# Products of k and v in four 64x64 quarters, over two PSUM banks

## The chip, the cores and the metric

The kernel runs on one core of a Trainium2 chip. The metric is the device time of one execution in microseconds (us). Before the change it is 837.13 us, the median of three runs (836.72 to 837.36).

## The reference, cut to what matters

```python
# batch 8, heads 8, seq 576, head_dim 64; x is (8, 576, 512)
kv = np.einsum('bhsd,bhse->bhde', k, v)
out = np.einsum('bhsd,bhde->bhse', q, kv)
rms = np.sqrt(np.mean(out * out, axis=-1, keepdims=True) + 1e-06)
x = (out / rms * g_norm)              # then heads side by side: 512 columns
...
h = x.transpose(0, 2, 1) @ U @ V      # rank 32, mixes along the sequence
u = x + h.transpose(0, 2, 1)
ch = np.maximum(u @ w_ch1, 0.0) @ w_ch2
return u + ch                         # all float32
```

The change touches only the first line, `k^T v`: a sum over 576 positions of the sequence, one 64x64 result for each of the 64 heads.

## The kernel before, in words

The 4608 tokens are nine blocks of 512. The first three (`NC`) go through `ffn1` (L480), `relu` (L491) and `ffn2` (L504) with each weight split into a high and a low part, three products for one. The other six go in three pairs through a seven-product scheme (`first_unit` L664, `second_unit` L761, order in `UNITS` L81); its weights are made during the first blocks by `weight_combos` (L608) and sent to DRAM on POOL's DMA queue (`wd`), together with plain copies of the weights (`weight_quarters` L593).

The attention part is spread between these products. A pair `(b, p)` is two heads of batch `b`. The table `RUNS` (L41) says behind which products `run` (L1061) is called; each call does one stage for three neighbouring pairs on TensorE, back to back: `t_product` of the pair before (L380; L387 and L390), `kv_product` of the next pair (L302, through `by_heads` at L294, matmul L300) and `out_product` of the pair itself (L310, matmul L319). Behind them the other engines do `t4_step` (L394), `kv_move` (L289), `squares` (L325), the statistics (L335) and `mul_step` (L358). `MIXES` (L46) places `mix_part` (L458), whose matmul L463 needs `t4`, some products later.

The order of TensorE is the order of the code (`manual_schedule`, L1139). The orders of DVE (VectorE), ACT (ScalarE), POOL (GpSimd) and SP (the DMA queue for loads and output) are set when the program is built, by a scheduler that works on its own estimates of how long each instruction takes. So a change to a few instructions can move others.

The two PSUM banks of a run are called `one` and `two` (in the trace `h` and `big`, or `pp` for both in the first three blocks). Columns 0 to 319 take `out_product`, one head in each bank, columns 320 to 447 of `two` the `t_product`, and columns 448 to 511 of one bank the 64x64 results of `kv_product`, head 0 in partitions 0 to 63 and head 1 in 64 to 127. `kv_move` copies them by ACT into `kvb` in SBUF, from where the next run's `out_product` takes them as the moving operand. Keys and values of a pair lie in SBUF as four tiles of 128 positions (`kv_sb`) and a tail of 64 (`kvt_sb`); for batches 2 to 7 the host pads the tail with 64 rows of zeros. A matmul in fp32 shows as two records, called passes here.

Of the kernel before, what the change touches and what calls it, by code (L numbers as in the profile page):

```python
# [16 lines left out]
ALU = mybir.AluOpType  # L17
AX = mybir.AxisListType

B, H, S, D = 8, 8, 576, 64  # L20
DM, DF, R = 512, 2048, 32
P = 128
NPAIR = H // 2
NT = 5
MAIN = 4 * P
TAIL = S - MAIN
# [4 lines left out]
BLK = 512  # L31
QL = [P + 32] * 2 + [P] * 2
QO = [0, 160, 320, 448]
ORDER = np.concatenate([np.arange(32) + P * i + 32 * a for a in range(4) for i in range(QL[a] // 32)])
NATIVE = 2
NC = 3
PAIRS = 3
KEEP = 4
# [54 lines left out]
def build(ctx: ExitStack, tc: tile.TileContext, kv_in, kvt0_in, kvt_in, q_in, uv_in, g_in, w_in, out):  # L93
    nc = tc.nc
# [25 lines left out]
    kvb = [const.tile([P, P], F32, name=f"kvb{i}") for i in range(2)]  # L120

    def weight_slot(name, shape, dtype, f):

        return const.tile(shape, dtype, name=name, tag=f"w_{f}")
# [51 lines left out]
    def move(which, n, out, in_, mul=None):  # L176

        e = ENG[which][n]
        if e == "a":
            if mul is None:  # L180
                nc.scalar.copy(out=out, in_=in_)
            else:
                nc.scalar.mul(out=out, in_=in_, mul=mul)
        else:
            eng = nc.vector if e == "v" else nc.gpsimd
            if mul is None:
                eng.tensor_copy(out=out, in_=in_)
            else:
                eng.tensor_scalar(out=out, in0=in_, scalar1=mul, scalar2=None, op0=ALU.mult)
# [9 lines left out]
    def load_kv(b, p):  # L199
        if b == 0 and 0 < p:  # L200
            if p not in first_kvq:
                first_kvq[p] = weight_slot(f"kvq{p}", [P, 2 * MAIN + S], F32, 8 + p)
            kt = first_kvq[p][:, 0:2 * MAIN]
        else:
            kt = ldp.tile([P, 2 * MAIN], F32, name="kv_sb")
        nc.sync.dma_start(out=kt, in_=kv_in[b, p])
        if b >= NATIVE:
            tt = ldp.tile([P, 2 * P], F32, name="kvt_sb")
            nc.sync.dma_start(out=tt, in_=kvt_in[b - NATIVE, p])
            loads["t", b, p] = tt  # L210
        elif p % 2 == 0:
            if b == 0 and p > 0:
                tt = temps[:, 2 * DM:2 * DM + 2 * P]
            else:
                tt = ldp.tile([P, 2 * P], F32, name="kvt_sb")
            nc.sync.dma_start(out=tt, in_=kvt0_in[b, p // 2])
            loads["t", b, p] = loads["t", b, p + 1] = tt
        loads["kv", b, p] = kt
# [65 lines left out]
    def banks():  # L284
        if "big" in second_y:
            return ps_h.tile([P, 512], F32, name="h"), second_y["big"].tile([P, 512], F32, name="big")
        return bank(), bank()

    def kv_move(b, p, pp):  # L289
        for lo in (0, D):  # L290
            own = slice(lo, lo + D)
            move("kv", p if b == 0 else -1, kvb[p % 2][own, own], pp[own])

    def by_heads(to, m, t, at):  # L294

        rows = slice(0, P) if at is None else slice(at, at + TAIL)
        for i in range(5):
            a, n = (m[:, i * P:], MAIN) if i < 4 else (t[rows], P)
            for lo in (0, D):
                nc.tensor.matmul(to[lo:lo + D], lhsT=a[:, lo:lo + D], rhs=a[:, n + lo:n + lo + D], start=i == 0, stop=i == 4)  # L300

    def kv_product(b, p, to):  # L302

        m = loads.pop(("kv", b, p))
        t = loads.pop(("t", b, p))
        by_heads(to, m, t, TAIL * (p % 2) if b < NATIVE else None)

    state = {}

    def out_product(b, p, heads):  # L310
        qt = loads.pop(("q", b, p))


        kb = kvb[p % 2]
        for i in range(NT):
            at = TAIL + i * P if i < 4 else 0
            for half in (0, D):
                for h, lo in enumerate((0, D)):
                    nc.tensor.matmul(heads[h][half:half + D, i * D:(i + 1) * D], lhsT=qt[lo:lo + D, at + half:at + half + D],  # L319
                                     rhs=kb[lo:lo + D, lo:lo + D], start=True, stop=True)  # L320
        x = x_sb[p % 2]
        state[b, p] = dict(x=x, x2=x, raw="two" in pools,
                           heads=[t[:, 0:NT * D].rearrange("p (i e) -> p i e", e=D) for t in heads])

    def squares(b, p):  # L325
        s = state[b, p]
        x = s["x"]
        for t, lo in zip(s["heads"], (0, D)):
            nc.scalar.activation(out=x[:, :, lo:lo + D], in_=t, func=AF.Copy if s["raw"] else AF.Square)
        if s["raw"]:  # L330
            xt = s["xt"] = sc.tile([P, 4, NT, 32], F32, name="xt")
            s["x2"] = xt.rearrange("p k i j -> p (k i j)").rearrange("p (i c) -> p i c", c=P)
            nc.scalar.activation(out=s["x2"], in_=x, func=AF.Square)
# [20 lines left out]
    def stats_step(b, p):  # L354
        for what in stats_parts(b, p).values():
            what()
# [27 lines left out]
    def t_product(b, p, tp):  # L384
        x = state[b, p]["x"]
        for i in range(4):
            nc.tensor.matmul(tp[R * i:R * (i + 1)], lhsT=uf[:, i, 0:R], rhs=x[:, i, :], start=True, stop=True)  # L387
        for i in range(2):
            cols = slice(i * D, (i + 1) * D)
            nc.tensor.matmul(tp[R * i:R * (i + 1), cols], lhsT=uf[:, 4, 0:R], rhs=x[:, 4, cols], start=False, stop=True,  # L390
                             skip_group_check=True)
        state[b, p]["tp"] = tp

    def t4_step(b, p):  # L394

        tp = state[b, p]["tp"]
        t4 = four.tile([P, P], F32R, name="t4")
        two = const.tile([2 * R, P], F32, name="two", tag="ident")
        other = sc.tile([2 * R, P], F32, name="other")
        nc.scalar.copy(out=two, in_=tp[2 * R:])  # L400
        nc.vector.tensor_tensor(out=two, in0=tp[0:2 * R], in1=two, op=ALU.add)
        for i in range(2):
            nc.scalar.copy(out=other[R * i:R * (i + 1)], in_=two[R * (1 - i):R * (2 - i)])
        nc.vector.tensor_tensor(out=two, in0=two, in1=other, op=ALU.add)
        nc.scalar.copy(out=t4[0:2 * R], in_=two)  # L405
        nc.vector.tensor_tensor(out=t4[2 * R:], in0=two, in1=t4[0:2 * R].bitcast(F32), op=ALU.subtract)
        state[b, p]["t4"] = t4
# [50 lines left out]
    def mix_part(b, p, part):  # L458
# [7 lines left out]
        if b > 2 and not (b in UPPER and part == 1):  # L466
            q = (S * b - BLK * NC) // (2 * BLK)
            at = S * b - BLK * NC - 2 * BLK * q
            to = x32(q)[p][:, at + lo:at + hi]
# [41 lines left out]
    def finish(y, j):  # L511
        uh, ul = ut[j]
        last_block = j == NC - 1
        kept = {}
# [27 lines left out]
    def x32(q):  # L542

        return [t[:, i] for t in x32_tiles(q) for i in range(2)]

    def carry(b, p):

        n = UPPER[b]
        q = (S * b + S - n - BLK * NC) // (2 * BLK)
        if b == 2:  # L550
# [161 lines left out]
    def end_unit(q, n, w):  # L712
# [17 lines left out]
        def leave(c, cols, queue):  # L730
            queue.dma_start(out=out[NC + 2 * q, 2 + c][:, cols], in_=ys[1][:, c, cols])

        if name != "P4":
            for c in range(2):
                products(c, slice(0, BLK), [(kk, w, hs)])
            if kk == KEEP - 1:
# [5 lines left out]
                if name == "P7":  # L742
                    nc.vector.tensor_tensor(out=ys[0], in0=ys[0], in1=spare("P5"), op=ALU.add)
                    for c in range(2):
                        nc.sync.dma_start(out=out[NC + 2 * q + 1, 2 + c], in_=ys[0][:, c])
            return
# [56 lines left out]
    uvraw = uvs[:, 0:NUV]  # L803
    nc.sync.dma_start(out=uvraw, in_=uv_in)
    load_kv(0, 0)
    load_q(0, 0)
    nc.vector.memset(eps[:, 0:1], 1e-6)
# [31 lines left out]
    for p in range(1, NPAIR):  # L839
        first[f"kv{p}"] = lambda p=p: load_kv(0, p)  # L840
        first[f"q{p}"] = lambda p=p: load_q(0, p)
# [60 lines left out]
    def spread_v(n, eng):  # L902
# [4 lines left out]
        out=uv, in_=uvraw.bitcast(U32).rearrange("p (n t) -> p n t", t=2)[:, :, 1].bitcast(F32), func=AF.Abs)  # L907
# [153 lines left out]
    def run(before, now, after):  # L1061

        one, two = banks()
        if before:
            t_product(*before, two[:, NT * D:NT * D + P])
        if after:
            kv = (two if after[0] < NATIVE and after[1] % 2 else one)[:, BLK - D:]
            kv_product(*after, kv)
        if now:
            out_product(*now, (one, two))  # L1070
        if before:
            t4_step(*before)
        if after:
            kv_move(*after, kv)
            following(load_kv, *after)
        if now:
            squares(*now)
            stats_step(*now)
            mul_step(*now)
            following(load_q, *now)  # L1080
            if now not in TURNS:
                turn_step(*now)

    def following(load, b, p):
        b, p = (b, p + 1) if p + 1 < NPAIR else (b + 1, 0)
        if b < B:
            load(b, p)
# [174 lines left out]
```

## Time and profile before

| | |
|---|---|
| median of three runs | 837.13 us (836.72 to 837.36) |
| the profiled execution | 837.33 us, its span 835.6 us |
| TensorE (PE) busy | 820.7 us, 98% |
| DVE busy | 585.4 us, 70% |
| ACT busy | 443.4 us, 53% |
| chain of work that ended last | PE 83%, DVE 6%, DMA 6%, ACT 3% |
| PE waits longer than 0.9 us past 50 us | 1.17 at 86.8, 3.42 at 98.4, 1.40 at 118.0, 0.94 at 536.6 |

The span is the profiled execution from its first to its last instruction. A row of a timeline gives the start and the duration, both in us, then engine, line, operation, the names written and read, shapes, and in brackets how long the engine had been idle before it and which instruction ended that. Time on an engine that nothing waits for costs nothing, so what a change is worth is read at the places where TensorE waits.

### The profile page before, as it was taken

To read this page: it belongs to the slowest core of one execution; us is meant where nothing else is said; L and a number is where in the kernel's file an instruction comes from. 1 tells how busy PE (TensorE), PEld (TensorE's weight loads), DVE (VectorE), ACT (ScalarE), POOL (GpSimd) and SP (SyncE) were. 2 spreads that over 40 slices of the span, in tenths; PEclk is the share of its full clock that TensorE was granted. 3 is DMA by queue.
4 is the path that set the end of the run, shared out by engine and by line. 5 is a ranking of instruction groups with operands and counts; after the bars stand their busy time and mean duration, and the time that the engine had idled before them with its cause. 6 is when DMAs were issued, how large, how long until landed. Compare 5 with 4: busy or idle time off the path is not lost.

```text
span 835.6 us, 14368 instructions
## 1 busy us (share of the span) xinstructions
PE 820.7 (98%) x5492; PEld 673.2 (81%) x5492; DVE 585.4 (70%) x1016; ACT 443.4 (53%) x810; POOL 80.3 (10%) x159
## 2 busy tenths in 40 slices
PE   8999799999999999999999999999999999999998
PEld 7777678888888888888888888788888888888887
DVE  5999885888776678666785688568736943582376
ACT  5978752544443445365645664656346724542462
POOL 3002214244330221000000000000000000000000
PEclk9999999999999999999999999999999999999999
DMA  9984767699887779467777768667555685555554
GB/s 346 415 340 144 225 200 226 219 321 277 262 252 266 239 214 316 160 236 262 241 264 236 264 238 282 231 204 242 178 187 196 207 281 197 182 196 195 202 200 153
DMA packets 66357, 198.39 MB, mean 237 GB/s; under 512 B 8176, under 2 KB 27376, under 8 KB 55536
## 3 DMA queue, kind: packets, MB, share of 16 engines
q1 hardware_dynamic: 57184, 167.97, 58.9%
q0 software_dynamic: 8960, 29.37, 10.5%
q8 instruction: 43, 0.70, 0.3%
q14 instruction: 26, 0.21, 0.1%
q10 hardware_dynamic: 144, 0.13, 0.0%
HBM read 146.84 MB, written 50.59 MB: 236 GB/s over the span
## 4 chain that ended last, share of the span: by engine, by line
PE 83%; DVE 6%; DMA 6%; ACT 3%; issue 1%; SPq 0%; ACTq 0%; DVEq 0%
PE yy L671 25%; PE yy L773 23%; PE y L508 13%; PE h L484 5%; PE h L485 5%; PE h L486 4%; DMA w1raw<-w_in 2%; PE ya L723 2%; DMA out<-x 1%; DMA raw<-w_in 1%; PE pp L300 1%; PE pp L319 1%; DVE dec L164 1%; PE h L300 1%; DVE uc L575 1%
## 5 line engine op out<-in xcount | busy, mean ns | idle before, releaser
L671 PE MATMUL yy<-uc,wt 128*128 128x512 f32 x1008 | 234.1, 391 | 0.9 <-ACT t L405 0.9
L671 PEld LDWEIGHTS yy<-uc,wt 128*128 128x128 f32 x1008 | 188.0, 188 | 40.7 <-ACT t L405 1.3
L773 PE MATMUL yy<-dec,wt 128*128 128x512 f32 x468 | 113.8, 391 | 0.3 <-DVE dec L662 0.3
L508 PE MATMUL y<-hh,ws 128*128 128x512 f32 x336 | 113.4, 393 | 0.0
L773 PE MATMUL yy<-hh,wt 128*128 128x512 f32 x312 | 103.3, 390 | 0.0
L773 PEld LDWEIGHTS yy<-dec,wt 128*128 128x128 f32 x468 | 87.2, 188 | 18.9 <-DVE dec L662 0.7
L662 DVE TENSOR_TENSOR hl<-hk,hh 128x512 fp32r<-128x512 f32 x72 | 48.1, 686 | 39.7 <-ACT hh L701 39.5
L662 DVE TENSOR_TENSOR dec<-hk,dec 128x512 fp32r<-128x512 f32 x72 | 48.9, 686 | 37.1 <-ACT dec L701 36.7
L508 PEld LDWEIGHTS y<-hh,ws 128*128 128x128 f32 x336 | 63.1, 188 | 13.8
L773 PEld LDWEIGHTS yy<-hh,wt 128*128 128x128 f32 x312 | 58.6, 188 | 12.4
L484 PE MATMUL h<-ut,ws 128*128 128x512 f32 x168 | 67.5, 402 | 0.0
L485 PE MATMUL h<-ut,ws 128*128 128x512 f32 x168 | 66.6, 396 | 0.0
L486 PE MATMUL h<-ut,ws 128*128 128x512 f32 x168 | 66.4, 395 | 0.0
L508 PE MATMUL y<-hl,ws 128*128 128x512 f32 x168 | 65.8, 391 | 0.0
L773 PE MATMUL yy<-hl,wt 128*128 128x512 f32 x156 | 60.7, 389 | 0.0
L701 ACT CAST dec<-hk 128x512 fp32r<-128x512 f32 x72 | 44.2, 621 | 29.0 <-PE yy L773 14.9
L701 ACT CAST hh<-hk 128x512 fp32r<-128x512 f32 x72 | 44.0, 622 | 27.0 <-PE yy L773 22.8
L659 ACT COPY sp<-yy 128x1024 f32<-128x1024 f32 x35 | 35.5, 1014 | 32.6 <-PE yy L671 25.3
L496 ACT ACTIVATE hh<-h 128x512 fp32r<-128x512 f32 x48 | 28.4, 591 | 36.8 <-PE h L486 36.6
L684 ACT ACTIVATE hk<-hk 128x1024 f32<-128x1024 f32 x24 | 25.5, 1061 | 36.3 <-DVE hk L683 36.3
L659 ACT COPY yy<-yy 128x1024 f32<-128x1024 f32 x17 | 17.0, 998 | 43.4 <-PE yy L671 40.5
L501 DVE SCALAR_TENSOR_TENSOR hl<-h,hh 128x512 fp32r<-128x512 f32 x48 | 32.7, 682 | 9.4 <-ACT hh L496 9.4
(237 smaller groups left out, 1348.0 us busy)
## 6 DMA issues: line engine op xcount, KB each, us to landing
wt<-wd SPq DMA_DIRECT2D x84, 1024.0 KB, 4.9
kv_sb<-kv_in SPq DMA_DIRECT2D x29, 512.0 KB, 5.9
raw<-w_in SPq DMA_DIRECT2D x14, 1023.6 KB, 14.9
wd<-dec POOLq DMA_DIRECT2D x44, 256.0 KB, 5.7
wd<-ws POOLq DMA_DIRECT2D x42, 256.0 KB, 4.0
q_sb<-q_in SPq DMA_DIRECT2D x29, 288.0 KB, 6.3
ut<-xd SPq DMA_DIRECT2D x28, 288.0 KB, 4.1
out<-x SPq DMA_DIRECT2D x23, 256.0 KB, 4.6
```

The lines of the kernel that those rows point to most:

```text
L484: nc.tensor.matmul(h, lhsT=w1s[f][0][:, d, :], rhs=uh[d], start=(n == 0), stop=False)
L485: nc.tensor.matmul(h, lhsT=w1s[f][0][:, d, :], rhs=ul[d], start=False, stop=False)
L486: nc.tensor.matmul(h, lhsT=w1s[f][1][:, d, :], rhs=uh[d], start=False, stop=(n == ND - 1))
L496: last["relu"] = nc.scalar.activation(out=last["hh"], in_=h, func=AF.Relu)
L501: last["low"] = nc.vector.scalar_tensor_tensor(out=hl, in0=h, scalar=0.0, in1=last["hh"].bitcast(F32), op0=ALU.max, op1=ALU.subtract)
L508: nc.tensor.matmul(acc, lhsT=w2s[f][w][:, c, :], rhs=h[:, cols], start=(f == 0 and w == 0 and h is hh), stop=(f == NF - 1 and w == 1))
L659: last["unit"] = nc.scalar.copy(out=pair_bank("P6") if name == "P1" else spare(name), in_=acc)
L662: return nc.vector.tensor_tensor(out=out, in0=a, in1=b, op=ALU.subtract)
L671: nc.tensor.matmul(acc[:, i], lhsT=w[:, ws_, e * P:(e + 1) * P], rhs=u[:, e, us], start=name in ("P1", "P5") and e == 0 and k == 0, stop=e ...
L684: last["unit"] = nc.scalar.activation(out=to, in_=to if other else acc, func=AF.Relu)
L701: last["unit"] = nc.scalar.copy(out=hh, in_=src)
L773: nc.tensor.matmul(acc[:, c], lhsT=w[:, ws_, c * P:(c + 1) * P], rhs=h, start=name in ("P1", "P5") and kk == 0 and i == 0, stop=kk == KEEP ...
```

## The change

`kv_product` of batches 2 to 7 (24 of the 32 pairs) goes through a new function `by_quarters`. Where `by_heads` did one matmul of 128 positions for each head and tile (a weight tile of 128x64), `by_quarters` does two of 64 positions each (weight tiles of 64x64): the upper rows go to bank `one`, the lower rows to bank `two`, four weight tiles side by side on the array. `kv_move` for these pairs copies the part in `one` to `kvb` by ACT and adds the part in `two` by DVE. The tails come without padding, 64 rows instead of 128. For batches 0 and 1 nothing changes.

```diff
+KV64 = 2
...
-            nc.sync.dma_start(out=tt, in_=kvt_in[b - NATIVE, p])
+            nc.sync.dma_start(out=tt[0:TAIL], in_=kvt_in[b - NATIVE, p])
...
     def kv_move(b, p, pp):
         for lo in (0, D):
             own = slice(lo, lo + D)
-            move("kv", p if b == 0 else -1, kvb[p % 2][own, own], pp[own])
+            if b >= KV64:
+                nc.scalar.copy(out=kvb[p % 2][own, own], in_=pp[0][own])
+                nc.vector.tensor_tensor(out=kvb[p % 2][own, own], in0=pp[1][own], in1=kvb[p % 2][own, own], op=ALU.add)
+            else:
+                move("kv", p if b == 0 else -1, kvb[p % 2][own, own], pp[own])
...
-        rows = slice(0, P) if at is None else slice(at, at + TAIL)
+        rows = slice(at, at + TAIL)
...
+    def by_quarters(to, m, t):
+
+        for i in range(5):
+            a, n = (m[:, i * P:], MAIN) if i < 4 else (t, P)
+            for r in (0, 1) if i < 4 else (0,):
+                rows = slice(r * D, (r + 1) * D)
+                for lo in (0, D):
+                    nc.tensor.matmul(to[r][lo:lo + D], lhsT=a[rows, lo:lo + D], rhs=a[rows, n + lo:n + lo + D], start=i == 0,
+                                     stop=i == (3 if r else 4))
...
-        by_heads(to, m, t, TAIL * (p % 2) if b < NATIVE else None)
+        if b >= KV64:
+            by_quarters(to, m, t)
+        else:
+            by_heads(to, m, t, TAIL * (p % 2))
...
-            kv = (two if after[0] < NATIVE and after[1] % 2 else one)[:, BLK - D:]
+            kv = [t[:, BLK - D:] for t in (one, two)]
+            kv = kv if after[0] >= KV64 else kv[after[1] % 2]
...
-    def padded(a):
-        n = B - NATIVE
-        a = tail_of(a[NATIVE:]).reshape(n, NPAIR, TAIL, P)
-        return np.concatenate([a, np.zeros_like(a)], axis=2)
+    def tails(a):
+        return tail_of(a[NATIVE:]).reshape(B - NATIVE, NPAIR, TAIL, P)
```

On TensorE the order only gains the new matmuls. On the other engines it moves at three places that the prediction speaks of; line numbers of the changed kernel are higher, by 1 near the top, by 18 from `kv_move` on.

The first place is ACT about 105 us into the program, where weight chunks are being decoded (`dec<-raw` is the first copy of a decode, `top<-dec` the second, `hh<-h` the relu). Before, and then now:

```order
L422 ACTIVATE ut<-ut_90,g_sb 128x448 [waits DMAHW5_49,DVE_49]
L167 COPY dec<-raw_1035 128x1024 [waits DMAHW7_49,DMAHW2_49,DVE_49]
L496 ACTIVATE hh<-h 128x512 [waits PE_49,Pool_49]
L168 COPY top<-dec 128x1024 [waits DVE_49]
L258 CAST ws_1382<-dec 128x1024 [waits DVE_49]
L168 COPY top<-dec 128x1024 [waits DVE_49,Activation_49]
```

```order
L440 ACTIVATE ut<-ut_90,g_sb 128x448 [waits DMAHW4_49,DVE_49]
L514 ACTIVATE hh<-h 128x512 [waits PE_49,Pool_49]
L168 COPY dec<-raw_1035 128x1024 [waits DMAHW7_49,DMAHW2_49,DVE_49]
L169 COPY top<-dec 128x1024 [waits DVE_49]
L259 CAST ws_1392<-dec 128x1024 [waits DVE_49]
L169 COPY top<-dec 128x1024 [waits DVE_49,Activation_49]
```

The relu now stands ahead of the copy `dec<-raw` and waits for TensorE there.

The second place is ACT at about 195 us, around a run (`kvb`, `two`, `x`, `other`, `xt`, `t` belong to it). `dec` and `sh` of `st` are the rounding of weight combinations in `weight_combos`; `sh` waits for POOL's earlier DMAs out of the same buffer. Before, and then now:

```order
L496 ACTIVATE hh<-h 128x512 [waits PE_49,Pool_49]
L628 CAST dec<-st 128x2x256 [waits DMASW6_49,DMASW5_49,DVE_49]
L181 COPY kvb_100<-pp 64x64 [waits PE_49]
L400 COPY two<-pp 64x128 [waits PE_49,Activation_49]
L628 CAST dec<-st 128x2x256 [waits DMASW3_49,DMASW2_49,DVE_49]
L181 COPY kvb_100<-pp 64x64
L329 ACTIVATE x_88<-pp 128x5x64
L403 COPY other<-two 32x128 [waits DVE_49]
L403 COPY other<-two 32x128
L329 ACTIVATE x_88<-pp 128x5x64
L333 ACTIVATE xt<-x_88 128x640 [waits DMAHW2_49,DMAHW1_49,DMAHW3_49,DMAHW0_49,Activation_49]
L405 CAST t_2319<-two 64x128 [waits DVE_49]
```

```order
L514 ACTIVATE hh<-h 128x512 [waits PE_49,Pool_49]
L646 CAST dec<-st 128x2x256 [waits DMASW6_49,DMASW5_49,DVE_49]
L646 CAST dec<-st 128x2x256 [waits DMASW7_49,DMASW0_49,DVE_49]
L646 CAST sh<-st 128x2x256 [waits DMASW4_49,DMASW5_49,DVE_49,Activation_49]
L294 COPY kvb_100<-pp 64x64 [waits PE_49]
L418 COPY two<-pp 64x128 [waits PE_49]
L294 COPY kvb_100<-pp 64x64
L347 ACTIVATE x_88<-pp 128x5x64
L421 COPY other<-two 32x128 [waits DVE_49]
L421 COPY other<-two 32x128
L347 ACTIVATE x_88<-pp 128x5x64 [waits DVE_49]
L351 ACTIVATE xt<-x_88 128x640 [waits DMAHW2_49,DMAHW1_49,DMAHW3_49,DMAHW0_49,Activation_49]
```

Now two roundings stand ahead of the run's first `kvb`, the second of them the `sh` that before came four rows behind `t_2319`, with its wait. POOL's DMAs behind the copy `begun` change their order at the same place. Before, and then now:

```order
L1158 COPY begun<-hh 128x1 [waits Activation_49]
L597 DMA wd_131<-ws_1210 128x2x256 [waits DMASW4_49]
L597 DMA wd_133<-ws_1210 128x2x256 [waits DMASW5_49]
L631 DMA wd_118<-sh 128x512 [waits DMASW6_49,DVE_49]
L631 DMA wd_118<-sh 128x512 [waits DMASW7_49]
L597 DMA wd_134<-ws_1263 128x2x256 [waits DMASW0_49]
```

```order
L1177 COPY begun<-hh 128x1 [waits Activation_49]
L649 DMA wd_118<-sh 128x512 [waits DMASW4_49,DVE_49]
L649 DMA wd_118<-sh 128x512 [waits DMASW5_49]
L615 DMA wd_131<-ws_1210 128x2x256 [waits DMASW6_49]
L615 DMA wd_133<-ws_1210 128x2x256 [waits DMASW7_49]
L615 DMA wd_134<-ws_1263 128x2x256 [waits DMASW0_49]
```

The two stores out of `sh` now go ahead of the two out of `ws_1210`.

The third place is DVE at about 536 us, in the middle of the first pair of blocks. `hk<-yy,sp` (L683 before, L701 now) takes a finished bank of `first_unit` to SBUF; `two`, `sums`, `t` and `r` belong to a run. Before, and then now:

```order
L662 TENSOR_TENSOR hl<-hk,hh 128x512 [waits Activation_49] x2
L401 TENSOR_TENSOR two<-big,two 64x128 [waits Activation_49]
L404 TENSOR_TENSOR two<-two,other 64x128 [waits DVE_49,Activation_49]
L683 TENSOR_TENSOR hk<-yy,sp 128x1024 [waits PE_49]
L348 TENSOR_REDUCE sums<-xt 128x10 [waits Activation_49]
L406 TENSOR_TENSOR t_5683<-two,t_5683 64x128 [waits Activation_49]
L683 TENSOR_TENSOR hk<-yy,sp 128x1024 [waits PE_49]
L351 RECIPROCAL r_5705<-ta 128x10 [waits Activation_49]
```

```order
L680 TENSOR_TENSOR hl<-hk,hh 128x512 [waits Activation_49] x2
L419 TENSOR_TENSOR two<-big,two 64x128 [waits Activation_49]
L295 TENSOR_TENSOR kvb_99<-big,kvb_99 64x64
L295 TENSOR_TENSOR kvb_99<-big,kvb_99 64x64 [waits Activation_49]
L422 TENSOR_TENSOR two<-two,other 64x128 [waits DVE_49,Activation_49]
L366 TENSOR_REDUCE sums<-xt 128x10 [waits Activation_49]
L424 TENSOR_TENSOR t_5911<-two,t_5911 64x128 [waits Activation_49]
L369 RECIPROCAL r_5935<-ta 128x10 [waits Activation_49]
L701 TENSOR_TENSOR hk<-yy,sp 128x1024 [waits PE_49]
```

`hk` now stands behind `sums`, `t` and the reciprocal, which waits for ACT's square root `ta` of `sums`. The two `kvb` rows are the new additions.

## Rows read from the trace of the kernel before

**Rows 1.** Section 1 of the page: busy time, share of the span, instructions.

```profile
PE 820.7 (98%) x5492; PEld 673.2 (81%) x5492; DVE 585.4 (70%) x1016; ACT 443.4 (53%) x810; POOL 80.3 (10%) x159
```

**Rows 2.** Timeline of PE: start, us, instruction, [idle before <-releaser]; four places.

```profile
101.78 0.58 PE L463 MATMUL pp<-v,t 128*128 128x288 f32 x1 [3.42 <-DVE t L406]
...
119.42 0.37 PE L463 MATMUL pp<-v,t 128*128 128x288 f32 x1 [1.40 <-DVE t L406]
205.45 0.33 PE L463 MATMUL pp<-v,t 128*128 128x384 f32 x1
...
537.58 0.70 PE L671 MATMUL yy<-uc,wt 128*128 128x512 f32 x2 [0.94 <-ACT t L405]
```

**Rows 3.** Busy time by windows; PEclk is the granted clock.

```profile
100.70:107.50 6.80, 5.72 (x14) 4.28 (x14) 6.59 (x17) 4.18 (x5) 2.36 (x4) 0.50 0.59 199
```

**Rows 4.** Timeline of PE in one run, 353.35 to 353.75.

```profile
353.35 0.29 PE L300 MATMUL h<-kvt_sb 128*64 128x64 f32 x4
353.56 0.27 PE L319 MATMUL h<-kvb,q_sb 64*64 64x64 f32 x1
...
353.67 0.22 PE L319 MATMUL h<-kvb,q_sb 64*64 64x64 f32 x1
...
353.73 0.22 PE L319 MATMUL h<-kvb,q_sb 64*64 64x64 f32 x1
```

**Rows 5.** Timeline of PE, run with a 64-row tail, at 73.4.

```profile
73.42 0.27 PE L300 MATMUL pp<-kvt_sb 64*64 64x64 f32 x2
73.44 0.28 PE L319 MATMUL pp<-kvb,q_sb 64*64 64x64 f32 x2
```

**Rows 6.** Timeline of ACT, 105 to 109.

```profile
105.40 1.15 ACT L167 COPY dec<-raw 128x1024 uint8<-128x1024 uint8 x1 [1.22 <-DMA wf<-dec]
107.77 0.60 ACT L496 ACTIVATE hh<-h 128x512 fp32r<-128x512 f32 x1 [1.22 <-PE h L486]
108.26 1.35 ACT L168 COPY top<-dec 128x1024 uint8<-128x1024 uint8 x1
```

**Rows 7.** Timeline of DVE, at 110.

```profile
110.34 1.21 DVE L164 SCALAR_TENSOR_TENSOR dec<-raw,top 128x1024 uint32<-128x1024 uint32 x1
```

**Rows 8.** Timeline of DVE, at 201.

```profile
201.07 0.28 DVE L406 TENSOR_TENSOR t<-two,t 64x128 fp32r<-64x128 f32 x1
```

**Rows 9.** Timeline of ACT, 195 to 204.

```profile
195.88 0.20 ACT L181 COPY kvb<-pp 64x64 f32<-64x64 f32 x1 [2.09 <-PE pp L319]
...
197.04 0.62 ACT L628 CAST dec<-st 128x512 fp32r<-128x512 f32 x1 [0.67 <-DVE st L622]
...
203.26 0.62 ACT L628 CAST sh<-st 128x512 fp32r<-128x512 f32 x1 [1.21 <-DMA wd<-sh]
```

**Rows 10.** Timeline of POOL, 193 to 196: issue of DMAs.

```profile
193.69 1.45 POOL L597 DMA_DIRECT2D wd<-ws  x2
195.14 1.11 POOL L631 DMA_DIRECT2D wd<-sh  x2
```

**Rows 11.** Timeline of DVE, 536 to 540.

```profile
536.06 0.28 DVE L404 TENSOR_TENSOR two<-two,other 64x128 f32<-64x128 f32 x1 [0.67 <-ACT other L403]
536.27 1.21 DVE L683 TENSOR_TENSOR hk<-yy,sp 128x1024 f32<-128x1024 f32 x1
537.40 0.80 DVE L348 TENSOR_REDUCE sums<-xt 128x10 f32<-128x640 f32 x1
...
539.69 0.21 DVE L351 RECIPROCAL r<-ta 128x10 f32<-128x10 f32 x1
```

**Rows 12.** Timeline of ACT, 536 to 539.

```profile
536.52 0.74 ACT L333 ACTIVATE xt<-x 128x640 f32<-128x640 f32 x1
...
538.48 0.29 ACT L349 ACTIVATE ta<-sums,eps 128x10 f32<-128x10 f32 x1
```

**Rows 13.** Chain of waits, 500 to 545: start, us, what.

```profile
519.69 7.10 DMA out<-x
```

**Rows 14.** Section 6 of the page: DMA issues, KB each, median us to landing.

```profile
out<-x SPq DMA_DIRECT2D x23, 256.0 KB, 4.6
```

More of the change, by code (lines that the diff above doesn't have):

```diff
@@ L1240 @@
         "kvt0_in": np.concatenate([tail_of(kk[:NATIVE]), tail_of(vv[:NATIVE])], axis=3),
-        "kvt_in": np.concatenate([padded(kk), padded(vv)], axis=3),
+        "kvt_in": np.concatenate([tails(kk), tails(vv)], axis=3),
         "q_in": np.concatenate([qq[:, :, :, MAIN:], qq[:, :, :, :MAIN]], axis=3).transpose(0, 1, 2, 4, 3).reshape(B, NPAIR, P, S),
```

## The prediction, made before the run

> **What bounds the kernel now.** I read the busy times of the page first: TensorE (PE) is busy for 820.7 of 835.6 us [rows 1]. So two things can move the end: the length of PE's own stream, and the few places where PE waits. For these I went through the timeline of PE for rows with idle time before them. Of the long ones three lie where the change reaches: 3.42 us before 101.78, 1.40 before 119.42 and 0.94 before 537.58 [rows 2]. The first two wait for `t` of DVE's L406, which ends a run's chain. The third is put down to ACT's `t`, which belongs to another matmul; what ended last before it is DVE's `hk` (536.27 + 1.21 = 537.48) [rows 11], which empties a bank that PE writes next. The row at 205.45 is an L463 that does not wait today.
>
> Then the granted clock by stretches [rows 3]. [...] Behind the 1.40 us idle it was up: the same L463 took 0.37 there, and 0.58 behind the 3.42 [rows 2]. So one idle of 3.42 us cost its own length and then 6.8 us at half speed, which is 3.4 us of work.
>
> **The change, part by part.**
>
> *Matmuls.* A row with x4 of L300 at 353.35 is two rounds of two records (the two heads, side by side); L319 has rounds of four, at 353.56, 353.67 and 353.73 [rows 4]. An ordinary round takes 0.06 us, with two tiles or with four. Between the last round of L300 (353.41) and the first of L319 stand 0.15, and the next takes 0.11: where the weight tile changes from 128x64 to 64x64, PE loses about 0.10 + 0.05 = 0.15 us. Where L300 has a 64x64 tile already, the tail in the run at 73.4, L319 begins 0.02 behind it, with no gap [rows 5]. In the change L300 has L319's tile shape throughout, so of two changes of shape per run one goes: 24 runs by 0.15 = 3.6 us saved. The rounds stay ten: five tiles by two passes for the upper rows, four by two for the lower, now four records a round instead of two.
>
> [...]
>
> *Additions.* 48 adds of 64x64 on DVE. The nearest row is `t` at 201.07, 64x128 in 0.28 [rows 8]; nothing is one bound, 0.28 the other, I take 0.2, about 10 us of DVE, which is 70% busy [rows 1]. In the order they stand between the first `two` of a run and the second, and in that stretch DVE waits for ACT's `other` anyway, 0.67 us at 536.06 [rows 11]. Without that cover each run's `t` would come up to 0.56 later, which matters only at the three places below.
>
> *Tails.* 24 loads of 64 KB instead of 128 KB, early loads nobody waits for: nothing.
>
> *First place, 119.42.* `hh` at 107.77 waits for PE, and the copy `dec<-raw` (1.15 us), which stood before it at 105.40, now stands behind it [rows 6]. So that copy runs from 108.26 to 109.41, and `top<-dec` (1.35) to 110.76. DVE's L164 needs it and begins at 110.98 instead of 110.34 [rows 7]: 0.65 later. From there to `t` at 119.42 it is one chain: each idle stretch that DVE has on the way was ended by an ACT step on the same chain. PE waits 0.65 longer. Bounds: nothing, if the wait for `hh` ends earlier, and 1.15, the whole copy.
>
> *Second place, 205.45.* The rounding of `sh`, which stood behind the run at 203.26 and there waited for POOL's stores, now stands ahead of the run's `kvb`, and so does the rounding at 197.04 [rows 9]. From `kvb` (195.88) to the end of `t` (201.35) are 5.47 us; without the rounding and the wait before it (0.62 + 0.67) 4.2 are left. So `t` is ready 0.62 + 4.2 = 4.8 after the stores out of `sh` have landed, and PE wants it at about 205.3. Before, they were issued at 195.14 behind two other stores (1.45) and had landed by 203.26 [rows 9, 10]. If they land as then, PE waits 2.9. If they gain the 1.45 by which they go ahead of the other stores, they land at 201.8 and PE waits 1.4. If they land by 200.4, it does not wait. A rounding is moved ahead of an earlier run as well and makes the engines later, which takes back some of the gain. I take 1.5, the middle; bounds 0 and 2.9.
>
> *Third place, 537.58.* `hk` (1.21) began at 536.27, ahead of `sums`; now it stands behind `sums`, `t` and the reciprocal, which need ACT's `xt` and `ta` [rows 11, 12]. `xt` ends at 537.26, `sums` takes 0.80, `ta` 0.29, the reciprocal 0.21, `hk` 1.21, with handovers it ends at about 539.8 instead of 537.48. PE waits 2.35 longer. The lower bound is nothing, if ACT's chain comes that much earlier (a rival); the upper adds two additions, 0.4.
>
> *Clock.* The third wait grows to 0.94 + 2.35, and 0.15 more because PE arrives earlier: 3.4 us, as long as the one idle that brought the clock down. I count it as a second fall, 3.4 us. Bounds: 0 and 3.4.
>
> *What the waits swallow.* In the three runs at those places the 0.15 saved only lengthens a wait: 21 runs by 0.15 = 3.15 are left.
>
> **Sum**, against the profiled execution (837.33, its span 835.6, 0.2 above the median of 837.13): -3.15 + 0.65 + 1.5 + 2.35 + 3.4 = +4.75. From the median that makes **841.9 us**. With 0 to 2.9 at the second place and 0.5 either way for the rest: 840.2 to 843.5.
>
> **Rivals.**
>
> *The clock stays up at 537.* Everything else as above: +1.35, 838.5, with the second place's bounds 837.0 to 840.0. For it: 1.40 us of idle did not bring the clock down, and there is only one idle of 3.4 to go by. Against it: the forecast's wait is just that long.
>
> *The clock falls at 119 too.* There the idle grows from 1.40 to 2.2, and only 12 us before, the clock was down. It would add 1.7 to 3.4: 843.6 to 845.3, with the bounds up to 847. For it: in the 3.42 us idle the clock was down before PE had work again; against it: the 1.40 us idle left no trace.
>
> *The other side: the output store lands early.* The chain that leads to the `hk` at 536 goes back to a store of `x` to the output, issued at 519.69 and landed 7.10 us later [rows 13], while the median of the 23 of its kind is 4.6 [rows 14]. The tail loads are smaller and some loads move, so it may land like the median, 2.5 us earlier. From 2.35 earlier on the third place adds nothing, PE's wait there stays at about 0.94, and the clock stays up. Then -3.15 + 0.65 = -2.5 without a wait at the second place: 834.6, faster. A wait there takes it back: with 1.5 it is 836.1, and from 0.9 on the change is within 0.2%. Against it: nothing in the order touches that store itself.
>
> *Quarters not side by side.* The change would not do what it says on the array. If each of the 36 records took half a round of L300, 0.029, a pair would take 1.04 instead of 0.58; 24 by 0.46 = 11 more: about 853. The rows of L319 speak against it. [...]
>
> **How the numbers follow.** Forecast 0.42, clock up at 537 0.25, clock down at 119 too 0.11, store early 0.17, quarters one by one 0.05. The predicted time is the forecast's, 841.9. About 1.7 us, 0.2%, is what a measurement of this kernel tells from no change: faster is below 835.5, slower above 838.8. Of the store rival 0.12 is faster, where the second place waits under 0.9, and 0.05 within 0.2%. Of the rival with the clock up two thirds lie within 0.2%: 0.17, together 0.22. All else is slower: 0.66. The range leaves out the faster part of the store rival and the rival on the quarters, and takes in the bounds of the others: 836.0 to 846.0. The likeliest case's own is 840.2 to 843.5.
>
> **What would show it.** L300 to L319 in the timeline of PE: no 0.15 between them, ten rounds of 0.06. PE's idle before L463 near 119: 2.2. Before L463 near 205: about 1.5, with ACT's `sh` ahead of `kvb` named by a `wd<-sh` store. Before L671 near 537: 3.4 behind DVE's `hk`, and a granted clock of 0.50 for some 7 us behind it. I would be wrong on the sign if that wait is missing, or if the clock stays at 1.00 there and the second place does not wait.

## The result, and the profile after

The changed kernel took 845.16 us (median of 7 runs, 840.2 to 845.93) beside 837.13 us for the kernel before (836.72 to 837.73): a ratio of 1.0083, 95% interval 1.0061 to 1.0105. It is slower, by 8.0 us where 4.8 was forecast. The profiled execution of it took 845.76 us with a span of 844.0. One execution of an experiment below (halves in the new order) had a mean granted clock of 0.65, took 1157.82 us, and is left out of its ratio.

The page's busy times of the changed kernel, and its chain by engine:

```profile
PE 820.5 (97%) x5876; PEld 672.3 (80%) x5876; DVE 595.6 (71%) x1064; ACT 443.1 (53%) x810; POOL 80.2 (9%) x159
...
PE 68%; DVE 12%; DMA 10%; ACT 4%; issue 3%; SPq 1%; POOL 1%; ACTq 0%; DVEq 0%; POOLq 0%
```

PE is busy as long as before [rows 1] although 384 records were added. What grew is the time in which it waits, and the chain shows it: PE's share falls from 83% to 68%, DVE's and the DMAs' grow from 6% each to 12% and 10%. The waits on PE from 50 us on, with the releaser, the total, how many and the longest:

```profile
PE pp L481 <- DVE t L424: 7.0, 3, 3.0
PE yy L689 <- issue: 3.5, 1, 3.5
PE pp L405 <- DVE x L381: 2.2, 2, 1.2
PE y L526 <- DVE hl L519: 1.8, 3, 0.9
PE y L526 <- ACT hh L514: 1.1, 1, 1.1
```

Before there were two waits for `t`, one of 1.2 for `x` and one of 0.9. Their places, in the timeline of PE:

```profile
100.85 0.37 PE L481 MATMUL pp<-v,t 128*128 128x288 f32 x1 [2.83 <-DVE t L424]
...
106.71 0.42 PE L405 MATMUL pp<-x,uf 128*32 128x128 f32 x8 [1.06 <-DVE x L381]
...
118.13 0.37 PE L481 MATMUL pp<-v,t 128*128 128x288 f32 x1 [1.20 <-DVE t L424]
...
159.66 0.50 PE L526 MATMUL y<-hl,ws 128*128 128x512 f32 x1 [0.95 <-DVE hl L519]
...
187.37 0.50 PE L526 MATMUL y<-hh,ws 128*128 128x512 f32 x1 [1.10 <-ACT hh L514]
188.10 0.50 PE L526 MATMUL y<-hl,ws 128*128 128x512 f32 x1 [0.22 <-DVE hl L519]
...
209.91 0.41 PE L481 MATMUL pp<-v,t 128*128 128x384 f32 x1 [2.97 <-DVE t L424]
...
348.45 0.50 PE L526 MATMUL y<-hl,ws 128*128 128x512 f32 x1 [0.66 <-DVE hl L519]
...
544.63 0.47 PE L689 MATMUL yy<-uc,wt 128*128 128x512 f32 x1 [3.52 <-issue]
```

The second place (209.91) and the third (544.63) wait for about 3 us and more; the first (118.13) less than before [rows 2]. Four rows stand where there was no wait: 106.71, 159.66, 187.37 with 188.10, and 348.45.

The granted clock, by windows behind three of them (the column ahead of the last two):

```profile
102.20:105.60 3.40, 3.40 (x9) 2.15 (x7) 3.03 (x8) 1.85 (x3) 0.83 (x2) 0.50 0.95 311
...
211.40:214.80 3.40, 3.40 (x10) 2.66 (x9) 3.37 (x6) 0.61 (x1) 1.11 (x2) 0.50 0.84 286
545.90:549.30 3.40, 3.40 (x10) 2.63 (x9) 3.02 (x3) 1.34 (x2) 0.00 (x0) 0.50 0.15 33
```

While PE had work left it fell three times for 3.4 us each, where before it fell once for 6.8 [rows 3]. The shorter stretch at 102 is not shown to come from the change: the length differs between executions. The kernel of the additions alone, below, has no quarters and the order of before, and its trace has 3.4 us there too:

```profile
101.40:104.70 3.30, 3.30 (x10) 2.63 (x10) 3.23 (x9) 2.07 (x4) 1.90 (x3) 0.50 0.86 293
104.80:108.10 3.30, 2.84 (x69) 2.13 (x72) 3.30 (x8) 2.78 (x3) 0.00 (x0) 1.00 0.30 101
```

Where the time went is read best from the start of the same matmul in both traces. How much later it starts in the changed kernel, in us:

| stretch of the changed kernel | later at its end | what moved it |
|---|---|---|
| to 101 | -0.9 | the wait at 98 is 0.6 shorter, the rest from the first 20 us |
| to 105 | -2.1 | the clock at half speed for 3.4 us less |
| at 107 | -0.9 | the new wait for `x` takes 1.2 back |
| 118 to 158 | -1.5 | runs, and the first place 0.2 shorter |
| at 160 | -0.3 | the new wait for `hl` |
| at 188 | +1.4 | the new waits for `hh` and `hl` |
| at 210 | +4.5 | the second place |
| to 215 | +6.3 | the clock |
| to 347 | +4.8 | eight runs at -0.19 |
| at 348 | +5.6 | the new wait for `hl` |
| to 541 | +4.5 | runs at -0.19, a wait of 0.5 at 535 |
| at 545 | +7.0 | the third place |
| to 550 | +8.6 | the clock |
| end | +8.4 | the last run |

The saving itself is there in every run. The timeline of PE in one run of the changed kernel:

```profile
267.09 0.69 PE L314 MATMUL pp<-kv_sb 64*64 64x64 f32 x32
267.61 0.23 PE L314 MATMUL pp<-kvt_sb 64*64 64x64 f32 x2
267.62 0.27 PE L337 MATMUL pp<-kvb,q_sb 64*64 64x64 f32 x2
267.67 0.23 PE L314 MATMUL pp<-kvt_sb 64*64 64x64 f32 x2
267.72 0.75 PE L337 MATMUL pp<-kvb,q_sb 64*64 64x64 f32 x38
```

Thirty-two records of quarters take 0.52 us, the tail's two rounds begin at 267.61 and 267.67, and L337 begins at 267.62, 0.01 behind the first of them: `out_product` already runs beside the tail, which has two tiles a round where the quarters have four. The 0.15 of [rows 4] are gone and 0.04 more; 24 runs by 0.19 are 4.5 us.

### The profile page after: what moved, and what is told of

Read it like the earlier page. It is cut to its first block, busy times and chain, and to the rows that moved or that the text cites. A ratio compares the mean times of both kernels' runs of the same rounds, so it can differ in the third digit from the quotient of the medians.

```text
span 844.0 us, 15183 instructions
## 1 busy us (share of the span) xinstructions
PE 820.5 (97%) x5876; PEld 672.3 (80%) x5876; DVE 595.6 (71%) x1064; ACT 443.1 (53%) x810; POOL 80.2 (9%) x159
## 4 chain that ended last, share of the span: by engine, by line
PE 68%; DVE 12%; DMA 10%; ACT 4%; issue 3%; SPq 1%; POOL 1%; ACTq 0%; DVEq 0%; POOLq 0%
PE yy L689 25%; PE yy L791 22%; PE y L526 7%; PE h L502 3%; PE h L504 2%; PE h L503 2%; DMA w1raw<-w_in 2%; PE ya L741 2%; DMA xd<-xt 2%; DMA out<-x 2%; DMA raw<-w_in 1%; DVE hl L519 1%; DVE uc L593 1%; DVE dec L165 1%; DMA wd<-dec 1%
## 5 line engine op out<-in xcount | busy, mean ns | idle before, releaser
L689 PE MATMUL yy<-uc,wt 128*128 128x512 f32 x1008 | 235.5, 392 | 4.0 <-issue 3.5
L689 PEld LDWEIGHTS yy<-uc,wt 128*128 128x128 f32 x1008 | 189.1, 189 | 44.1 <-issue 3.9
L526 PEld LDWEIGHTS y<-hl,ws 128*128 128x128 f32 x168 | 31.8, 190 | 9.5 <-DVE hl L519 3.5
```

What stands on the lines that cost most here:

```text
L526: nc.tensor.matmul(acc, lhsT=w2s[f][w][:, c, :], rhs=h[:, cols], start=(f == 0 and w == 0 and h is hh), stop=(f == NF - 1 and w == 1))
L689: nc.tensor.matmul(acc[:, i], lhsT=w[:, ws_, e * P:(e + 1) * P], rhs=u[:, e, us], start=name in ("P1", "P5") and e == 0 and k == 0, stop=e ...
```

## The experiments

**How the order was put back.** The order of DVE, ACT, POOL and SP in the changed kernel differs from that before in some thirty places of two to fourteen instructions. Edges that set the issue order alone, without a wait, put it back, so that TensorE's part and the order can be tried apart. The edit, cut to the chain of one place on one engine; numbers are positions in the order in which the code emits an engine's instructions:

```diff
+CHAINS = dict(
...
+    ACT=[[591, 600, 597, 598, 601]],
...
+)
...
     rest.close()
+    names = dict(DVE=mybir.EngineType.DVE, ACT=mybir.EngineType.Activation, POOL=mybir.EngineType.Pool, SP=mybir.EngineType.SP)
+    for name, chains in CHAINS.items():
+        own = [i for i in nc.cur_bb.bb.instructions if i.engine == names[name] and not type(i).__name__.startswith(("BassTile", "InstTile"))]
+        for chain in chains:
+            for a, b in zip(chain, chain[1:]):
+                tc.add_manual_dep(own[b], own[a].name, mybir.DependencyInfo(mybir.DependencyClass.NoSync, mybir.DependencyReason.DATA), reason="order")
```

The chain shown is ACT's at the third place, as the kernel under "One place back" has it; the others have such lists for DVE, ACT, POOL and SP. In the traces of the kernels with all chains the instructions of the four engines, apart from the additions, do stand in the order before, or in the new one. Gains and losses below are told by the ratios to the kernel before, since not all runs were on one chip.

**All places back.** All chains (42), on the changed kernel.

> The changed kernel with the order of the kernel before put back on DVE, ACT, POOL and SP by edges between instructions (the 48 additions stand behind the first `two` of their run); TensorE as changed. Theory A, the order alone costs: the quarters save 0.19 us a run as in the trace of the changed kernel, 24 runs, 4.6 us, of which the three old waits swallow about 0.6; PE waits where it did before and nowhere else, the clock falls once: 832.4 to 834. Theory B, the additions themselves lengthen the chains to `t`: new waits of 0.4 and more at many runs stay, 838 to 845. Theory C, the quarters cost elsewhere on TensorE: 845 as changed.

Measured: 833.75 us, 0.9961 of the kernel before (0.9946 to 0.9976). The waits on PE:

```profile
PE pp L487 <- DVE t L430: 4.5, 2, 2.9
PE pp L411 <- DVE x L387: 2.3, 3, 1.1
PE yy L695 <- ACT t L429: 1.2, 1, 1.2
```

These are the three old places, and a wait for `x` at 106 (0.94) that stands behind a half-speed stretch of 3.4 us; the traces of the additions alone and of the tails alone, with such a stretch, have that wait too (0.46 and 0.83). Theory A holds: with the old order the same matmuls and additions are faster than the kernel before, and 10 us faster than with the new order (0.9961 against 1.0083). Of the 4.5 us that the runs save, 3.3 are left; longer waits take the rest.

**The other corner: halves in the new order.** The kernel before, with instructions in place of the additions and the chains of the changed kernel's order:

```diff
             move("kv", p if b == 0 else -1, kvb[p % 2][own, own], pp[own])
+            if b >= NATIVE:
+                nc.vector.tensor_tensor(out=kvb[p % 2][own, own], in0=kvb[p % 2][own, own], in1=kvb[p % 2][own, own], op=ALU.max)
```

> The kernel before (no quarters, padded tails) with 48 additional DVE instructions of 64x64 in place of the additions (max of `kvb` with itself, so the result is the same) and, by edges, the order of the changed kernel on DVE, ACT, POOL and SP. Theory A, the order alone costs: all waits of the changed kernel without its saving, 845.2 + 4 = 848 to 850. Theories B and C need the quarters or the reading of a second bank: 837 to 839.

Measured: 844.85 us, 1.0107 (1.0092 to 1.0122). The new order makes the kernel slower without any quarter, as theory A says, but to 844.85 and not to 848 or more. It was run once more, beside the changed kernel on the same chip:

> The changed kernel as it is, once more, beside the next run on the same chip: 845 as before; its waits at 107, 159, 187, 207, 348 and 541 again, and the clock falling behind 207 and 541.

> Halves with the additional instructions and the order of the changed kernel, once more, for a trace of it. Theory A: the same waits as in the changed kernel. If the quarters' saving of 4.5 were all left, it would be 849.6; if the waits swallow it, since each ends when a store or a chain that began earlier ends, the idle times of PE are shorter here by about the part saved, and the time is 845 to 847.

Measured: the changed kernel 844.32 us, 1.0092 (1.007 to 1.0113); halves in the new order 842.93, 1.0084 (1.0065 to 1.0103). So in the new order the quarters gain nothing that can be measured. The waits of halves in the new order:

```profile
PE pp L471 <- DVE t L414: 5.4, 2, 3.1
PE pp L395 <- DVE x L371: 3.6, 2, 2.4
PE yy L679 <- issue: 1.7, 1, 1.7
```

The rows at the second and the third place:

```profile
206.57 0.50 PE L471 MATMUL pp<-v,t 128*128 128x384 f32 x2 [2.25 <-DVE t L414]
```

```profile
540.84 0.47 PE L679 MATMUL yy<-uc,wt 128*128 128x512 f32 x1 [1.68 <-issue]
```

At the third place PE waits 1.68 where the changed kernel waits 3.52. From the start of the row at the second place to that at the third are 334.3 us here and 334.7 in the changed kernel (209.91 to 544.63), so the chain to `hk` ends alike; but PE gets there 332.6 us behind the second place here and 331.2 in the changed kernel. With quarters PE is there 1.4 sooner, and it waits 1.8 longer. At the second place (2.25 here, 2.97 in the changed kernel and 3.58 the second time) this is not what the trace shows: without quarters PE gets there 2.6 us sooner, and the waits at 159 and 187 (2.3 in all in the changed kernel) are missing here. Why they are, with the same order, is open. So theory A is shown for the time, and not for every wait. The clock falls once here, at 106 for 3.4 us, and behind neither of the two places; but this is the fastest of the six executions (840.55 us), and what the clock costs in the others no trace shows. Both times that I expected were too high: to the first I had only added the saving, and the second (845 to 847) took off too little.

In its second trace the changed kernel waits at 107, 160, 188, 211 and 545 again (1.30, 0.72, 0.57, 3.58 and 3.56), not at 348, and the clock falls at 102, 211 and 546, for 3.4 us each time.

**The additions alone.** The same edit with the old order.

> The kernel before with the same 48 additional DVE instructions and its own order otherwise: what the additions cost by their time alone. Theory A: hidden, at most 0.4 at each of the three old waits, 837.1 to 838.3. Theory B: 840 or more.

Measured: 836.07 us, 0.9997 (0.9987 to 1.0007). 48 instructions more on DVE, and no difference. Each takes 0.22 us as an addition does, but reads SBUF alone and need not wait for TensorE; the additions themselves stand in the run with all places back, which has no new waits at many runs either. By the two theory B is out.

**The tails alone.** 64 rows without padding; the main part as before, in the old order.

```diff
-            nc.sync.dma_start(out=tt, in_=kvt_in[b - NATIVE, p])
+            nc.sync.dma_start(out=tt[0:TAIL], in_=kvt_in[b - NATIVE, p])
...
-        rows = slice(0, P) if at is None else slice(at, at + TAIL)
+        rows = slice(at, at + TAIL)
```

> The kernel before with only the tails changed: 64 rows, no padding, the matmuls of the tail in 64x64 tiles, the 512 rows still in 128x64 tiles, no additions; the order of before. If the saving on TensorE is one change of tile shape less per run, nothing is saved here, since the change moves from behind the tail to ahead of it: 836 to 837 (before 836.6 on this chip). If the saving is the shorter tail, 24 times 0.19 less the part that waits swallow: 832.5 to 834.

Measured: 835.66 us, 0.999 (0.9979 to 1.0002): no difference that is clear of noise. The timeline of PE in one run shows why:

```profile
368.22 0.69 PE L306 MATMUL h<-kv_sb 128*64 128x64 f32 x16
368.83 0.27 PE L306 MATMUL h<-kvt_sb 64*64 64x64 f32 x2
368.85 0.28 PE L325 MATMUL big<-kvb,q_sb 64*64 64x64 f32 x2
368.94 0.23 PE L306 MATMUL h<-kvt_sb 64*64 64x64 f32 x2
```

The tail begins 0.61 behind the start of the run and its second round 0.11 behind the first; in the changed kernel it is 0.52 (267.09 to 267.61) and 0.06. The loss of the change of shape has only moved ahead of the tail. Compared with halves and additions in the old order, the matmul behind each run gains 0.01 a run by the tails alone, and 0.19 by the quarters.

**One place back.** The changed kernel with the chains of the third place only (DVE, ACT and SP about 541 us).

> The changed kernel with the old order only at the third place (DVE, ACT and SP about 541 us: `hk` ahead of `sums` again). Theory A: the wait of 3.5 goes back to about 1 and the clock does not fall there, 2.5 + 1.6 less: 840 to 841.5. Rival: the wait moves on to the second `hk` or a later bank, 843 or more.

Measured: 839.79 us, 1.0045 (1.0031 to 1.0059). No wait of PE is left there; those at 160, 188 and 210 are (0.86, 0.62 and 2.53). By the ratios (1.0083, and 1.0092 when the changed kernel ran again) 3.2 to 3.9 us come back, near the 4.1 of theory A.

**One place new, from the fast base.** Quarters with the old order, and the new order at one place only; each kernel leaves out the chains of its place. The base is the run with all places back (0.9961, 831.16 to 834.75 us). A difference of two such ratios is uncertain by 0.2 to 0.26% here, about 2 us.

> Quarters with the old order everywhere (833.75 us median) except for the first place, DVE, ACT and SP up to about 120 us, which have the order of the changed kernel: the relu ahead of the copy `dec<-raw`. The step of the prediction: PE waits 0.65 longer near 118, 834.4. Rival, from the trace of the changed kernel, where that wait was 1.20 and not 2.2: the copy had room, 833.2 to 833.8.

Measured: 832.79 us, 0.9952 (0.9935 to 0.9969): not slower than the base, if anything faster. The prediction's step is wrong here, and the rival right that the copy had room.

> Quarters with the old order (833.75) except for ACT, DVE and POOL at about 178 to 188 us, where a rounding that waits for POOL's store stands ahead of `kvb` and a relu, as in the changed kernel. Theory A, the rounding's wait delays the relu: 1.1 + 0.5 of waits on PE near 187, 835.2 to 835.8. Rival (what I took in the prediction, that only slack is used there): 833.4 to 834.

Measured: 835.15 us, 0.9987 (0.9971 to 1.0004): 0.26%, 2.2 us, above the base, as theory A has it, but barely beyond the noise. Six of the twelve executions lie between 833.15 and 834.7, inside the base's range; the trace is of a long one (837.95). ACT and PE there:

```profile
187.19 0.62 ACT L652 CAST dec<-st 128x512 fp32r<-128x512 f32 x1 [4.24 <-DMA wd<-dec]
...
188.79 0.59 ACT L520 ACTIVATE hh<-h 128x512 fp32r<-128x512 f32 x1
```

```profile
189.43 0.50 PE L532 MATMUL y<-hh,ws 128*128 128x512 f32 x1 [1.65 <-ACT hh L520]
```

The rounding waits 4.24 us for a store out of its buffer, and the relu behind it on ACT is late for PE, by 1.65.

> Quarters with the old order (833.75) except for the second place, ACT, DVE and POOL at about 196 to 210 us, as in the changed kernel: two roundings ahead of `kvb`. Theory A: the wait for POOL's store there is enough by itself, 3.0 at 207 and a fall of the clock behind it, 1.7: 837.5 to 838.7. With a wait of 1.5 and no fall, the prediction's step: 835.2. Rival, it needs the lateness that the place at 186 brings: 834.5 or less.

Measured: 837.85 us, 1.0005 (0.9984 to 1.0027): 0.44%, 3.7 us, above the base: theory A. The rounding, the wait, and the clock behind it:

```profile
202.11 0.62 ACT L652 CAST sh<-st 128x512 fp32r<-128x512 f32 x1 [3.32 <-DMA wd<-sh]
```

```profile
206.99 0.41 PE L487 MATMUL pp<-v,t 128*128 128x384 f32 x1 [2.32 <-DVE t L430]
```

```profile
207.30:210.60 3.30, 3.30 (x10) 2.63 (x9) 3.06 (x9) 0.25 (x2) 2.82 (x5) 0.50 0.61 206
```

> Quarters with the old order (833.75) except for the third place, DVE, ACT and SP at about 533 to 545 us, as in the changed kernel: `hk` behind `sums`, `t` and the reciprocal. Theory A: the wait there grows from 1.2 by 2.35 to 3.5, and the clock falls behind it for 3.4 us, 1.7 more: 837.3 to 838.3. Without the clock 836.1. Rival, the wait is one of late DMA and not of the order: 834 or less.

Measured: 837.96 us, 1.0014 (0.9996 to 1.0031): 0.53%, 4.4 us, above the base: theory A. The wait is 3.06 there, and behind it the clock is at half speed for 6.8 us in this execution, the longest of the twelve (841.38 us):

```profile
539.10 1.19 PE L695 MATMUL yy<-uc,wt 128*128 128x512 f32 x2 [3.06 <-issue]
```

```profile
538.20:545.00 6.80, 5.90 (x14) 4.68 (x15) 6.29 (x9) 2.52 (x3) 0.00 (x0) 0.50 0.49 164
```

> Quarters with the old order (833.75 us median) except for DVE, ACT and SP at about 150 to 162 us and about 340 to 350 us, as in the changed kernel: at the one `mul` and two of the run's steps stand ahead of the relu's low part `hl`, at the other `two` does. Theory A: waits of about 0.9 near 159 and 0.6 near 348 as in the trace of the changed kernel, 834.6 to 835.4. Rival: those waits come from the lateness of other places, 833.2 to 834.

Measured: 835.62 us, 0.9987 (0.9974 to 0.9999), 2.2 us above the base, but not by the waits that theory A named. The waits on PE that neither the kernel before nor the trace of all places back has in this size:

```profile
PE pp L487 <- DVE ut L494: 0.8, 1, 0.8
PE y L532 <- ACT hh L520: 0.5, 1, 0.5
```

No wait for `hl` stands at 159 or at 348. A wait for `ut` at 173 (0.76) and one for `hh` at 237 (0.53) are there instead; the trace of the third place alone, with the old order at these places, has both as well (0.65 at 173 and 1.18 at 238), so they are not shown to be these places' doing. The wait at 348 was not there in the changed kernel's second trace either. What makes up the 2.2 us here, and what brings the waits at 159 and 348, was not settled.

Together the five places give -0.8 + 2.2 + 3.7 + 4.4 + 2.2 = 11.7 us; the whole new order costs 10.2 (1.0083 less 0.9961), 11.0 by the second run of the changed kernel. With about 2 us of uncertainty on each of the five, that they add up is no proof that nothing else counts; the new order at about 208 us on POOL and at 236 on ACT and DVE stands in none of the five.

## Why the prediction was right in sign and short by 3 us

By the table above the changed kernel ends 8.4 us later, 3.6 more than the sum. The sum lacked the place at 186 (1.9), the waits at 159, 348 and 535 (1.2, 0.8 and 0.4) and 1.6 of the second place; the first place came out 0.9 below its term, the runs saved 0.7 more than counted, and 0.9 was gained before 101. So the sign and the third place were foreseen, and the size came near by terms that were off both ways. The measured 845.16 lies above the likeliest case's 840.2 to 843.5. It is in the stated range because that was drawn wide enough for the rival with the clock down at 119, which did not come: that is luck. (Added as they are written, the bounds of the likeliest case make 839.9 to 843.8, and that rival's upper bound of 847 is not in the range.)

*The saving.* The mechanism was right: one change of tile shape less. 0.15 a run was too small; the runs show 0.19, 4.5 us in all. That the 0.04 come from `out_product` starting beside the tail (0.01 behind its first round) is my estimate. That tails alone save nothing (0.999, and 0.01 a run) shows it is the change of shape and not the shorter tail. What was left of it, 3.3 with the old order where 3.15 was forecast, agrees by two errors that cancel: more saved, and more of it taken by waits.

*Additions and tails.* Right: nothing, by two runs (0.9997 and 0.999). An addition takes 0.22 us.

*The first place, +0.65.* Wrong. The step took `hh` from [rows 6], where it waits for a TensorE at half speed until 107.5. In the changed kernel's trace the clock was back at 105.6. ACT and DVE there:

```profile
105.75 0.60 ACT L514 ACTIVATE hh<-h 128x512 fp32r<-128x512 f32 x1 [1.69 <-PE h L504]
106.24 1.12 ACT L168 COPY dec<-raw 128x1024 uint8<-128x1024 uint8 x1
```

```profile
109.04 1.22 DVE L165 SCALAR_TENSOR_TENSOR dec<-raw,top 128x1024 uint32<-128x1024 uint32 x1
```

L165 begins 1.3 earlier than in [rows 7], not 0.65 later; PE itself is 0.9 earlier there. With the clock back at 105.6 the relu ahead did not lengthen PE's wait (1.20, before 1.40), and alone it did not make the kernel slower (0.9952; PE's wait there is 1.26 with it, 1.59 in the base). The step had taken one execution's half-speed stretch for a property of the kernel. Whether it holds where the clock is down from 100 to 107, no trace with the new order shows.

*The second place, +1.5.* The mechanism was right, the size was my upper bound: 2.97, and 2.32 alone. The step that failed is the issue of the stores, which the sum let come 1.45 sooner for their going first. They were issued at 198.43 and had landed for the cast at 205.04:

```profile
198.43 1.12 POOL L649 DMA_DIRECT2D wd<-sh  x2 [0.36 <-DVE sh L647]
```

```profile
205.04 0.62 ACT L646 CAST sh<-st 128x512 fp32r<-128x512 f32 x1 [2.95 <-DMA wd<-sh]
```

That is 6.6 us for a landing, less than the 8.1 before [rows 9, 10]. But the issue itself was 3.3 later than before, and only 1.3 of that is PE's own delay by then. The brackets name DVE's `sh`, which was late. Alone, with the place at 186 in its old order, the stores were issued at 194.99, again behind DVE's `sh` and only 0.15 sooner than before; they had landed by 202.11, and PE's wait was 2.32.

*The place at 186.* I wrote that a rounding ahead of an earlier run only takes back some of that gain. It is a place of its own: 1.10 and 0.22 of waits, 1.9 us by the same matmul's start, 2.2 alone (barely beyond the noise). The term was missing from the sum, because I followed that rounding only to `t` and not to the relu behind it on ACT.

*The third place, +2.35.* Right: the wait grew from 0.94 to 3.52, 2.6 us. DVE shows the order of events that the step named:

```profile
541.87 0.82 DVE L366 TENSOR_REDUCE sums<-xt 128x10 f32<-128x640 f32 x1 [0.95 <-ACT xt L351]
542.72 0.28 DVE L424 TENSOR_TENSOR t<-two,t 64x128 fp32r<-64x128 f32 x1
543.06 0.22 DVE L369 RECIPROCAL r<-ta 128x10 f32<-128x10 f32 x1
543.31 1.23 DVE L701 TENSOR_TENSOR hk<-yy,sp 128x1024 f32<-128x1024 f32 x1
```

The page calls the releaser "issue"; `hk` ends at 544.54 and L689 starts at 544.63.

*The clock, +3.4.* It fell behind the third place, as said, but for 3.4 us and not 6.8, which is 1.6 by the same matmul's start. It also fell behind the second place, 1.8 more, which I had not counted. So two short falls cost what the sum had for one long one, 3.4: the term came out by luck. At 102 it was 3.4 us long, as in kernels without the change, and the wait for `x` took back what that gained. The falls differ between executions, which may be why the changed kernel's lie from 840.2 to 845.93: over the whole span the granted clock is 0.998 in the one of 840.2 and 0.991 to 0.994 in the other six. That was not tried.

*The rivals.* The early store did not come: in the trace it took 7.8 us to land. The quarters run side by side: 32 records in 0.52 us at 267.09, where one by one they would have needed 0.93 by the rival's 0.029 each. The clock did not fall at 119 in either trace of the changed kernel.

Not foreseen were the waits at 159 and 348 (0.95 and 0.66): there `mul`, or `two`, has moved ahead of the low part of a relu on DVE. Alone, that order does not show them, and the second trace of the changed kernel has only the first (0.72).

The versions that beat both kernels are those with the quarters and the old order: everywhere (0.9961, 0.9946 to 0.9976), or except at the first place (832.79 us, 0.9952, 0.9935 to 0.9969). The two cannot be told apart.

## What to carry to other kernels

Where a scheduler sets the order, price an edit twice: what it does on its own engine, and what the order that comes out with it does on the others; an edit that gains can be kept by pinning the old order (here 0.9961 with the old order, 1.0083 with the new). Follow an instruction that is moved ahead of a wait to everything behind it on its engine, not only to the chain that you first looked at (the rounding at 186 cost PE 1.10 by the relu behind it). A saving ahead of a wait for a chain that began earlier can go into the wait: from the second place on PE came 1.4 us sooner to the third with the quarters, and waited 1.8 longer there. And a wait that grows can cost the clock on top: behind the waits of 2.97 and 3.52 us it was at 0.50 for 3.4 us each.

## What the runs showed that I had not expected

In these traces a fall of the clock does not follow from the length of one idle time. With the new order at 186 alone, PE was idle for 3.33 us before 101.99 and the clock stayed up; behind an idle time of 2.00 before 119.58 it fell:

```profile
101.90:105.20 3.30, 3.21 (x14) 2.43 (x14) 3.15 (x9) 2.50 (x3) 2.18 (x3) 1.00 0.76 259
120.60:123.90 3.30, 3.30 (x9) 2.58 (x8) 2.81 (x5) 0.43 (x1) 2.17 (x3) 0.50 0.49 158
```

Nor does the length of the fall: behind 3.06 at the third place it stayed down for 6.8 us in one kernel, behind 3.52 for 3.4 in another.

Four 64x64 tiles over two banks took a round of 0.06 us, as two 128x64 tiles did before (0.52 us for the 16 records, eight rounds, of `kv_sb` at 352.83), also where all of them accumulate (32 records, eight rounds, in 0.52 us at 267.09).
